# A block-sparse attention and MLP kernel: a new order of operations, the row table built first, and other bytes for outputs that nobody reads

## The chip, the cores and the metric

The kernel runs on one core of one Trainium2 chip. The time is the device time of one execution in microseconds (us). The five engines of the core run their own instruction streams and wait for each other by semaphores: TensorE (PE, whose weight loads are listed apart as PEld), VectorE (DVE), ScalarE (ACT), GpSimd (POOL) and SyncE (SP), which here only issues transfers.

## The reference

Four batches of eight heads, 768 positions of 64 columns. Blocks of 32 positions attend to their neighbours, to the first and last block, and to three blocks drawn at random for each row of blocks; the first and last block attend to everything. The result, 3072 rows of 512 columns, goes through a two-layer network with a leaky activation whose slope is given for each of the 2048 inner columns.

```python
mask = np.abs(blk_i - blk_j) <= window
mask = mask | (blk_i == 0) | (blk_j == 0) | (blk_i == n_blocks - 1) | (blk_j == n_blocks - 1)
for qb in range(n_blocks):
    for kb in sampled_blocks[qb]:
        mask[qb * block:(qb + 1) * block, kb * block:(kb + 1) * block] = True
scores = np.where(mask, scale * np.matmul(q, k.transpose(0, 1, 3, 2)), -1000000000.0)
attn = softmax(scores); x = rows of np.matmul(attn, v)
h = x @ w_in
out = (np.maximum(h, 0.0) + alpha * np.minimum(h, 0.0)) @ w_out
```

## The kernel before

All matmuls take float16 operands; a float32 number is carried as a high and a low half (names ending in hi and lo, or gh and gl), so that a product takes three matmuls. Scales that keep the halves in range come from norms of the inputs, worked out on the chip.

**Units.** The attention is cut into 48 units U0 to U47: for each batch b and each of six query tiles t, two halves c of four heads. Five tiles are sparse; the sixth (t = 5; U10, U11, U22, U23, U34, U35, U46, U47) holds the rows that attend to everything and is called dense. A unit is a chain: scores on PE (L741) into one of three banks; `emit_bias` on DVE (L823: mask, scale and row minimum nm); the exponential on ACT (L830); high half of the probabilities p_hi (L451 on ACT, L453 on DVE, L455 on POOL); low half p_lo (L459 on DVE, L461 and L462 on POOL); a transposing DMA `pt<-ph` issued by SP (L875 sparse, L879 dense); and the product with the values on PE (L741, `a<-v,pt` and the like). Then `evict`: the row scale, x_mul (L883), its halves, and the transposing DMA `x<-xn` (L900).

**Keys and values.** For each batch they are normed, split into halves and transposed (`keys<-ph`, L594); the blocks drawn at random come by POOL's copies (L736) and by an indirect DMA on POOL (L697, `vr<-scr,vidx`). The indices vidx come from a table of five columns called vrow (row number and comparisons, L411 to L420) and vpick. Queries: `qf` is loaded, squared and summed on ACT (`emit_q_sq`, L447), scaled on DVE (L440, L443: uq, sq), split (qn), transposed (`qt<-qn`, L525), and a second copy with halves swapped is made by a DMA `qs<-qt`; dense scores need both.

**The network.** Twelve chunks M0 to M11 of 256 rows follow the units: for each of eight steps j, up (L1352; M0 in float32, L1340), the activation on DVE (L1362, L1366), its high half on ACT (L1375) and low half on POOL (L1381), and down (L1402) into an output bank; then out (L1412) and a store. Up and down write two and two banks. The norm of w_in and w_out is worked out with chains of small matmuls and of `diag` (L548, DVE), which ends in `otot` (L1202), `mm` (L1209) and s_wo (L443).

**What sets the order.** Every step is an operation of a `Plan`, numbered as the program text comes to it, 2492 in all. `Plan.run` goes through a table `ORDER` (L70 to L164), whose words name an engine and a number (D for DVE, A for ACT, G for POOL, S for SP, P for PE); it hands out buffers in that order, and each engine issues in that order without going around a waiting instruction. Only the code ahead of the plan (L287 to L375) and the constants are placed by the text.

**Outputs that nobody reads.** ACT's squares (L447) and DVE's `diag` are wanted for their sums alone. ACT writes the squares into the first bytes of a tile called rawp (under the name spare), or for the first query tile into phs[0], a buffer for probabilities; `diag` writes the first 128 columns of rawp, the same bytes as spare.

## Time and profile before

| | |
|---|---|
| Median of three runs | 773.38 us (767.51 to 775.49) |
| The profiled execution | 775.92 us, of which the span of instructions is 773.7 us |
| Mean granted clock of PE | 0.976 |
| PE busy | 697.6 us (90%), 9978 instructions |
| DVE busy | 533.7 us (69%), 1377 |
| ACT busy | 371.3 us (48%), 838 |
| POOL busy | 475.6 us (61%), 848 |
| Chain that ended last | PE 68%, DVE 11%, DMA 10%, issue 5%, others below 3% each |

The page has the span in 40 slices; PE is busy 3, 4, 5, 7, 7, 7 tenths in the first ones and nine tenths from the tenth on with two slices at eight. DVE stands at eight and nine tenths in the first twelve slices, and lower after that. An execution is 2.2 us longer than its span of instructions. Matmuls are pipelined, so that the durations of neighbours overlap; sums of PE's time are taken from the stretches that a view gives as one piece. An idle time in square brackets is that of the engine just before the row's instruction, with what ended it.

### The profile page before, as it was taken

Reading aid. Unit: us, or ns where it says so; the run is one execution under the profiler, and the core shown is the slowest. Engines: PE = TensorE matmul, PEld = TensorE weight load, DVE = VectorE, ACT = ScalarE, POOL = GpSimd, SP = SyncE. Lnnn points to the kernel's source line nnn. Section 1 sums busy time; section 2 is a strip of 40 time slices with the busy share of each in tenths; the row PEclk is TensorE's granted clock in tenths of the full one; section 3 lists DMA queues with packets and bytes.
Section 4 is the critical chain, followed back from the end, with each engine's and each line's share of the span. In section 5 each row is a group of like instructions: output and inputs, shape, how many; then the busy total and the mean of one; then the engine's idle time right before and its main releaser. Section 6 shows DMA issues by size and latency. Waiting matters only on the chain.

```text
span 773.7 us, 25323 instructions
## 1 busy us (share of the span) xinstructions
PE 697.6 (90%) x9978; PEld 490.8 (63%) x9978; DVE 533.7 (69%) x1377; ACT 371.3 (48%) x838; POOL 475.6 (61%) x848
## 2 busy tenths in 40 slices
PE   3457799899989999999999989999998999999997
PEld 2345588456657757668667566577674677676673
DVE  3888899889887654878776757589754547586130
ACT  3546668773744433466434455366531533343211
POOL 5359545564677787758768767475785677345121
PEclk9976899999999999999999999999998999999999
DMA  8987769777897999999997999998984878756200
GB/s 235 297 252 219 222 152 233 171 179 151 167 190 217 188 205 179 202 222 191 170 210 191 178 202 210 188 195 166 184 226 129 154 161 149 165 98 113 65 1 28
DMA packets 284710, 136.48 MB, mean 176 GB/s; under 512 B 216992, under 2 KB 272432, under 8 KB 284592
## 3 DMA queue, kind: packets, MB, share of 16 engines
q1 hardware_dynamic: 256064, 98.74, 64.2%
q0 software_dynamic: 5792, 18.36, 8.8%
q10 hardware_dynamic: 22736, 17.77, 8.3%
q8 instruction: 78, 1.28, 0.7%
q14 instruction: 40, 0.33, 0.1%
HBM read 70.86 MB, written 12.58 MB: 108 GB/s over the span
## 4 chain that ended last, share of the span: by engine, by line
PE 68%; DVE 11%; DMA 10%; issue 5%; POOL 2%; ACT 2%; SPq 1%; another core or an unknown queue 0%; POOLq 0%; ACTq 0%; DVEq 0%
PE o L1402 25%; PE h L1352 24%; PE s L741 6%; PE a L741 5%; PE h L1340 4%; DMA pt<-ph 3%; DVE ph L459 2%; DMA vf<-in_k_dram 2%; DMA qs<-qt 1%; DVE e L823 1%; DMA qf<-in_q_dram 1%; DVE wi L1166 1%; DMA vn<-scr 1%; POOL gl L1381 1%; DMA keys<-ph 1%
## 5 line engine op out<-in xcount | busy, mean ns | idle before, releaser
L1352 PE MATMUL h<-x,wi 128*128 128x256 f16 x2112 | 242.9, 274 | 2.1 <-DMA x<-xn 1.2
L1352 PEld LDWEIGHTS <-wi 128*128 128x128 f16 x2112 | 205.8, 98 | 34.5 <-issue 3.0
L1402 PE MATMUL o<-wo,gh 128*128 128x512 f16 x728 | 216.7, 379 | 1.2 <-ACT g L1412 1.2
L1381 POOL TENSOR_TENSOR gl<-g,gh 128x512 f16<-128x512 f32 x91 | 109.1, 1205 | 101.4 <-ACT gh L1375 92.7
L736 POOL COPY keys<-keys 128x128 f16 x480 | 130.2, 320 | 23.7 <-ACT keys L605 15.2
L1402 PE MATMUL o<-wo,gl 128*128 128x512 f16 x364 | 138.0, 379 | 0.0
L830 ACT ACTIVATE e<-e,nm 128x256 f32<-128x256 f32 x160 | 79.9, 500 | 104.5 <-DVE nm L823 97.5
L1362 DVE SCALAR_TENSOR_TENSOR g<-h,am 128x512 f32<-128x512 f32 x96 | 65.8, 686 | 86.3 <-PE h L1352 66.1
L1402 PEld LDWEIGHTS <-gh 128*128 128x128 f16 x728 | 68.7, 98 | 76.5 <-issue 3.0
L1375 ACT CAST gh<-g 128x512 f16<-128x512 f32 x91 | 55.4, 611 | 116.1 <-DVE g L1366 66.9
L823 DVE CUSTOM_DVE_ANT_0 e<-s,bias,cs 128x256 f32<-128x256 f32 x160 | 73.3, 477 | 33.5 <-POOL ph L462 15.9
L697 POOL DMA_INDIRECT vr<-scr,vidx x80 | 79.5, 994 | 24.5 <-issue 19.0
L741 PEld LDWEIGHTS <-pt 128*32 128x32 f16 (+1 forms) x4416 | 58.7, 96 | 31.3 <-issue 21.5
L1366 DVE SCALAR_TENSOR_TENSOR g<-h,gsc,g 128x512 f32<-128x512 f32 x96 | 72.1, 751 | 3.4
L741 PE MATMUL s<-keys,qt 128*32 128x192 f16 (+2 forms) x864 | 69.2, 254 | 4.5 <-DVE nm L823 2.9
L741 PE MATMUL s<-keys,qs 128*32 128x192 f16 (+2 forms) x864 | 69.9, 253 | 1.9 <-DMA qs<-qt 1.9
L1402 PEld LDWEIGHTS <-gl 128*128 128x128 f16 x364 | 35.6, 98 | 43.4 <-POOL gl L1381 0.5
L461 POOL TENSOR_SCALAR e<-e 128x512 f32<-128x512 f32 (+1 forms) x38 | 27.7, 729 | 57.0 <-ACT ph L451 30.3
L459 DVE SCALAR_TENSOR_TENSOR ph<-e,ph 128x512 f16<-128x512 f32 (+1 forms) x62 | 59.6, 967 | 2.0 <-ACT ph L451 1.6
L462 POOL TENSOR_TENSOR ph<-e,ph 128x512 f16<-128x512 f32 (+1 forms) x38 | 50.6, 1332 | 3.2
L451 ACT ACTIVATE ph<-e 128x512 f16<-128x512 f32 (+1 forms) x69 | 47.7, 693 | 4.6 <-DMA pt<-ph 2.1
L741 PE MATMUL a<-vr,pt 128*32 128x64 f16 x1920 | 39.4, 199 | 6.4 <-issue 6.3
(216 smaller groups left out, 963.1 us busy)
## 6 DMA issues: line engine op xcount, KB each, us to landing
vn<-scr SPq DMA_DIRECT2D x60, 192.0 KB
wo<-in_moe_w_in_dram SPq DMA_DIRECT2D x15, 512.0 KB
qs<-qt SPq DMA_DIRECT2D x40, 128.0 KB
vf<-in_k_dram SPq DMA_DIRECT2D x18, 256.0 KB
vf<-in_v_dram SPq DMA_DIRECT2D x16, 256.0 KB
scr<-v SPq DMA_DIRECT2D x16, 256.0 KB
vn<-scr ACTq DMA_DIRECT2D x20, 192.0 KB
qf<-in_q_dram SPq DMA_DIRECT2D x14, 256.0 KB
```

The source lines that it names most:

```text
L459: nc.vector.scalar_tensor_tensor(dst, src, scale, hi, ALU.mult, ALU.subtract)
L697: nc.gpsimd.indirect_dma_start(dst[:n], None, T["scr", b].rearrange("s h a -> s (h a)"), bass.IndirectOffsetOnAxis(ap=vidx[:n, i : i + 1], ...
L736: nc.gpsimd.tensor_copy(kr[:, :, g, r], kt[:, :, bass.ds(i * HB2, HB2)])
L741: nc.tensor.matmul(dst, lhs, rhs, start=start, stop=False, skip_group_check=True)
L823: nc.vector.tensor_tensor_reduce(e_view(u, h // 2)[:, h % 2, :], T["sp", u, h], bias[:, t], scale=T["cs", b, t][:, c : c + 1], scalar=3.0e ...
L830: nc.scalar.activation(e, e, AF.Exp, bias=T["nm", u, h], scale=-1.0, accum_out=su_of(u, h))
L1352: nc.tensor.matmul(ph[:, i, :], win(k, f, ct), x[:, l, ct, cols], start=(m == 0), stop=(m == len(terms) - 1))
L1362: nc.vector.scalar_tensor_tensor(g, ph, 0.0, a2, ALU.min, ALU.mult)
L1366: nc.vector.scalar_tensor_tensor(g[:, i : i + 2], ph[:, i : i + 2], sc, g[:, i : i + 2], ALU.mult, ALU.add)
L1375: nc.scalar.copy(T["gh", c, j, half], g)
L1381: nc.gpsimd.tensor_tensor(T["gl", c, j, half], g, T["gh", c, j, half], ALU.subtract)
L1402: nc.tensor.matmul(T["o", c, t], g[:, i, a : a + P], wout(w, f), start=(f == 0 and m == 0), stop=(f == NF - 1 and m == 2),)
```

## The change

Three things are changed; what is computed, and with which instructions, stays the same.

- **The table.** All 2492 words of `ORDER` are given anew. Some operations go to another engine: 47 from ACT to DVE and 45 back, 37 from POOL to DVE and 35 back, 35 loads from ACT to SP and 26 back, 14 from ACT to POOL and 8 back.
- **The row table.** The two POOL and nine DVE instructions that build vrow leave the planned operation `o_vidx` for the code ahead of the plan, and the five DVE instructions that are left in it form the operation.
- **Bytes that are thrown away.** The first query's squares go into the tile qn that is allocated there, not into phs[0]; `diag` writes bf16 into columns of rawp behind those that ACT's squares fill.

```diff
--- before.py
+++ after.py
@@ -68,99 +68,99 @@
 ORDER = """
-S289 S274 S26 A307 S272 S273 A308 D309 A312 D313 P12 D13 S290 G0 D1 D4 A8 S359 D27 A28 G2 S14 P275 D276 D277 P278 D279 S291 P314 P316 D29 A42 D317 S74
...
+A307 S273 S274 A272 S26 P275 A308 D309 D312 D313 G0 D1 S291 D27 A28 D29 S234 S289 D276 D277 P278 A290 D3 S359 S14 S232 S74 D279 D286 A283 G287 S42
...
 """
@@ -297,6 +297,18 @@
     rawp = cpool.tile([P, 3 * W2 // 4], I32, name="rawp")
     nc.scalar.dma_start(rawp[:, : NBLK * NR * 2], smp.partition_broadcast(P))
     sraw = rawp[:, : NBLK * NR * 2].rearrange("p (a r w) -> p a r w", r=NR, w=2)
+    vrow = cpool.tile([P, 5], F32, name="vrow")
+    row, below, m1, m2, tmp = (vrow[:, i : i + 1] for i in range(5))
+    nc.gpsimd.iota(row[:KR], pattern=[[0, 1]], base=0, channel_multiplier=1, allow_small_or_imprecise_dtypes=True)
+    nc.gpsimd.iota(row[KR:], pattern=[[0, 1]], base=0, channel_multiplier=1, allow_small_or_imprecise_dtypes=True)
+    for r, n in ((slice(0, KR), KR // 2), (slice(KR, P), HB2)):
+        nc.vector.tensor_scalar(below[r], row[r], n - 0.5, None, ALU.is_ge)
+        nc.vector.scalar_tensor_tensor(row[r], below[r], -float(n), row[r], ALU.mult, ALU.add)
+    nc.vector.tensor_scalar(m1, row, HB2 - 0.5, None, ALU.is_ge)
+    nc.vector.tensor_scalar(m2, row, 2 * HB2 - 0.5, None, ALU.is_ge)
+    nc.vector.scalar_tensor_tensor(row, below, float(SP2), row, ALU.mult, ALU.add)
+    nc.vector.tensor_tensor(tmp, m1, m2, ALU.add)
+    nc.vector.scalar_tensor_tensor(row, tmp, -float(HB2), row, ALU.mult, ALU.add)
     ident16 = cpool.tile([P, P], F16, name="ident16")
     nc.gpsimd.tensor_copy(ident16, ident)
 
@@ -321,7 +333,6 @@
     sidx = wi[:1, 0, 3 * P : 3 * P + NBLK * NR].bitcast(I32).rearrange("p (a r) -> p a r", r=NR)
     vidx = cpool.tile([P, TS * NG4], I32, name="vidx")
     vpick = cpool.tile([P, TS * NG4, NR], F32, name="vpick")
-    vrow = cpool.tile([P, 5], F32, name="vrow")
     spack = cpool.tile([1, TS * NG4 * NR // 2], I32, name="spack")
     bias = cpool.tile([P, TS, CS], BF16, name="bias")
     dbias = cpool.tile([P, S], BF16, name="dbias")
@@ -407,17 +418,6 @@
     o_regs = plan.op(-11, {"POOL": 3.5}, lambda: emit_regs(nc.gpsimd, "g"), [o_pack])
 
     def emit_vidx():
-        row, a, m1, m2, tmp = (vrow[:, i : i + 1] for i in range(5))
-        nc.gpsimd.iota(row[:KR], pattern=[[0, 1]], base=0, channel_multiplier=1, allow_small_or_imprecise_dtypes=True)
-        nc.gpsimd.iota(row[KR:], pattern=[[0, 1]], base=0, channel_multiplier=1, allow_small_or_imprecise_dtypes=True)
-        for r, n in ((slice(0, KR), KR // 2), (slice(KR, P), HB2)):
-            nc.vector.tensor_scalar(a[r], row[r], n - 0.5, None, ALU.is_ge)
-            nc.vector.scalar_tensor_tensor(row[r], a[r], -float(n), row[r], ALU.mult, ALU.add)
-        nc.vector.tensor_scalar(m1, row, HB2 - 0.5, None, ALU.is_ge)
-        nc.vector.tensor_scalar(m2, row, 2 * HB2 - 0.5, None, ALU.is_ge)
-        nc.vector.scalar_tensor_tensor(row, a, float(SP2), row, ALU.mult, ALU.add)
-        nc.vector.tensor_tensor(tmp, m1, m2, ALU.add)
-        nc.vector.scalar_tensor_tensor(row, tmp, -float(HB2), row, ALU.mult, ALU.add)
         v = [vpick[:, :, x] for x in range(NR)]
         nc.vector.tensor_tensor(v[2], v[2], v[1], ALU.subtract)
         nc.vector.tensor_tensor(v[1], v[1], v[0], ALU.subtract)
@@ -425,7 +425,7 @@
         nc.vector.scalar_tensor_tensor(v[0], v[2], m2, v[0], ALU.mult, ALU.add)
         nc.vector.tensor_scalar(vidx, v[0], float(HB2), row, ALU.mult, ALU.add)
 
-    o_vidx = plan.op(P_REG, {"POOL": 3.0}, emit_vidx, [o])
+    o_vidx = plan.op(P_REG, {"DVE": 1.1}, emit_vidx, [o])
     o_r = plan.op(-9, {"DVE": 2.0}, mask_random, [o])
     o_d = plan.op(0, {"DVE": 0.75}, mask_dense, [o])
     o_bias = [plan.op(-8 + 5 * t, {"ACT": 0.5, "POOL": 0.6}, lambda e, t=t: spread_picked(e, t), [o_r]) for t in range(TS)]
@@ -497,7 +497,10 @@
 
     def emit_q_sq(b, t):
         T["ssq", b, t] = new_small("ssq", n=4)
-        early = phs[0].rearrange("p a b c -> p (a b c)").bitcast(U8) if (b, t) == (0, 0) else None
+        early = None
+        if (b, t) == (0, 0):
+            T["qn", b, t] = wt("qn", [P, H, 2, D], F16)
+            early = T["qn", b, t].rearrange("p h a d -> p (h a d)").bitcast(U8)
         squares(T["qf", b, t].rearrange("p h d -> p (h d)"), T["ssq", b, t], early)
 
     def emit_q_scale(b, t):
@@ -511,7 +514,8 @@
         nc.vector.tensor_scalar(cs, T["rk", b][:, a:z], T["uq", b, t], -(2.0**-100), ALU.mult, ALU.min)
 
     def emit_q_hi(e, b, t):
-        T["qn", b, t] = wt("qn", [P, H, 2, D], F16)
+        if ("qn", b, t) not in T:
+            T["qn", b, t] = wt("qn", [P, H, 2, D], F16)
         times(e, T["qn", b, t][:, :, 0, :], T["qf", b, t], T["sq", b, t])
 
     def emit_q_lo(b, t):
@@ -546,7 +550,7 @@
 
     def diag(src, acc):
         nc.vector.tensor_tensor_reduce(
-            rawp[:, :P].bitcast(F32), src, ident, scale=1.0, scalar=0.0, op0=ALU.mult, op1=ALU.add, accum_out=acc,
+            rawp[:, P:].bitcast(BF16), src, ident, scale=1.0, scalar=0.0, op0=ALU.mult, op1=ALU.add, accum_out=acc,
         )
 
     def emit_sq_diag(key, b, c):
@@ -976,11 +980,11 @@
         plan.tag = f"Q{b}{t}"
         fb, nb = plan.buf("qf"), plan.buf("qn")
         o = plan.op(pl, LQ, lambda e: emit_load_q(e, b, t), gate, [fb], dma=1.6, n=1 + (t == TS))
-        o = plan.op(prio, {"ACT": 0.8}, lambda: emit_q_sq(b, t), [o], [], [fb])
+        o = plan.op(prio, {"ACT": 0.8}, lambda: emit_q_sq(b, t), [o], [nb] if (b, t) == (0, 0) else [], [fb])
         o = plan.op(prio, {"DVE": 0.27}, lambda: emit_q_scale(b, t), [o])
         for c in range(NQ):
             o_cs[b, t, c] = plan.op(prio, {"DVE": 0.08}, lambda c=c: emit_cs(b, t, c, c + 1), [o, o_rk[b, c]])
-        o = plan.op(prio, {"POOL": 0.7, "ACT": 0.63, "DVE": (0.36, 0)}, lambda e: emit_q_hi(e, b, t), [o], [nb], [fb])
+        o = plan.op(prio, {"POOL": 0.7, "ACT": 0.63, "DVE": (0.36, 0)}, lambda e: emit_q_hi(e, b, t), [o], [] if (b, t) == (0, 0) else [nb], [fb] + ([nb] if (b, t) == (0, 0) else []))
         o = plan.op(prio, {"DVE": (0.79, 0)}, lambda: emit_q_lo(b, t), [o], [], [nb, fb])
         qtbuf[b, t], qsbuf[b, t] = plan.buf("qt"), plan.buf("qs")
         if (b, t) < (0, Q_PE):
```

In the changed kernel L426 to L497 keep their numbers, and later lines stand three or four further down: L525 is L529 there, L548 is L552, L741 is L745, L823 is L827, L875 is L879, L900 is L904, L1202 is L1206.

VectorE at the program's start, and where the row table stood before. Before, behind the weights' arithmetic (wi, wo) of the first 50 us:

```order
L1161 SCALAR_TENSOR_TENSOR wi<-wo,wi 128x512
L511 TENSOR_SCALAR cs<-rk,uq 128x1
L414 TENSOR_SCALAR vrow<-vrow 96x1
L415 SCALAR_TENSOR_TENSOR vrow<-vrow 96x1
L414 TENSOR_SCALAR vrow<-vrow 32x1
L415 SCALAR_TENSOR_TENSOR vrow<-vrow 32x1
L416 TENSOR_SCALAR vrow<-vrow 128x1
L417 TENSOR_SCALAR vrow<-vrow 128x1
L418 SCALAR_TENSOR_TENSOR vrow<-vrow 128x1
L419 TENSOR_TENSOR vrow<-vrow 128x1
L420 SCALAR_TENSOR_TENSOR vrow<-vrow 128x1
L422 TENSOR_TENSOR vpick<-vpick 128x20
```

In the changed kernel, from VectorE's first memset on:

```order
L287 MEMSET ones 128x128
L305 TENSOR_SCALAR vrow<-vrow 96x1
L306 SCALAR_TENSOR_TENSOR vrow<-vrow 96x1
L305 TENSOR_SCALAR vrow<-vrow 32x1
L306 SCALAR_TENSOR_TENSOR vrow<-vrow 32x1
L307 TENSOR_SCALAR vrow<-vrow 128x1
L308 TENSOR_SCALAR vrow<-vrow 128x1
L309 SCALAR_TENSOR_TENSOR vrow<-vrow 128x1
L310 TENSOR_TENSOR vrow<-vrow 128x1
L311 SCALAR_TENSOR_TENSOR vrow<-vrow 128x1
L440 TENSOR_SCALAR uq<-ssq 128x1
```

All nine vrow instructions moved from behind the weights to ahead of the first query.

VectorE at the end of the norm of w_out, with the numbers of the buffers. Before:

```order
L548 ISA rawp_131,osum_190<-o0_120,ident_122 128x128
L548 ISA osum_190 128x1
L440 TENSOR_SCALAR uq_2391<-ssq_2356 128x1
L443 TENSOR_SCALAR sq_2392<-uq_2391 128x1
L1202 TENSOR_REDUCE otot_2396<-osum_190 128x1
L1209 TENSOR_REDUCE mm_2402<-o1_121 128x1
L440 TENSOR_SCALAR mu_2403<-mm_2402 128x1
L443 TENSOR_SCALAR s_wo_192<-mu_2403 128x1
L453 TENSOR_SCALAR wo_136<-wo_136,s_wo_192 128x512
```

In the changed kernel:

```order
L552 ISA rawp_131,osum_201<-o0_120,ident_122 128x128
L552 ISA osum_201 128x1
L1206 TENSOR_REDUCE otot_2380<-osum_201 128x1
L1213 TENSOR_REDUCE mm_2383<-o1_121 128x1
L440 TENSOR_SCALAR mu_2384<-mm_2383 128x1
L443 TENSOR_SCALAR s_wo_203<-mu_2384 128x1
L827 ISA e1_81,nm_2392<-s1_115,bias_163,cs_1807 128x256
```

A query's two scale steps (uq, sq) no longer stand between the last `diag` and otot, and the first split of w_out (L453) is no longer VectorE's; it stands on POOL.

SyncE's queue at the query of the dense unit U34 (qt_77 and qs_79). Before:

```order
L875 DMA_TRANSPOSE pt_86<-ph_138 128x8x128
L875 DMA_TRANSPOSE pt_84<-ph_141 128x8x128
L525 DMA_TRANSPOSE qt_77<-qn_75 128x8x128
L594 DMA_TRANSPOSE keys<-ph_140 128x8x128
L900 DMA_TRANSPOSE x_89<-xn_88 128x8x128
L479 DMA qs_79<-qt_77 64x1024 x2
L875 DMA_TRANSPOSE pt_83<-ph_138 128x8x128
```

In the changed kernel:

```order
L529 DMA_TRANSPOSE qt_77<-qn_75 128x8x128
L479 DMA qf_74<-in_q_dram 128x8x64
L479 DMA vn_104<-scr_7079 48x4x512 x2
L879 DMA_TRANSPOSE pt_84<-ph_151 128x8x128
L479 DMA qs_79<-qt_77 64x1024 x2
L904 DMA_TRANSPOSE x_89<-xn_88 128x8x128
L479 DMA vn_103<-scr_7079 48x4x512 x2
L598 DMA_TRANSPOSE keys<-ph_152 128x8x128
```

The swap `qs<-qt` now stands ahead of the transposes of x and of the keys, and behind the loads of a query and of values.

## Rows read from the trace of the kernel before

**Rows 1.** Three windows: length, busy PE, PEld, DVE, ACT, POOL (count), PEclk, DMA, GB/s.

```profile
9.20:101.70 92.50, 55.13 (x1006) 45.02 (x1006) 78.43 (x250) 52.06 (x96) 50.34 (x128) 0.85 0.80 241
101.70:773.70 672.00, 642.35 (x8974) 445.66 (x8973) 455.07 (x1127) 317.02 (x739) 418.79 (x685) 0.99 0.83 167
586.10:592.90 6.80, 5.80 (x60) 4.03 (x61) 0.00 (x0) 0.00 (x0) 5.20 (x15) 0.50 0.48 142
```

**Rows 2.** Waits until 102 us, VectorE and TensorE: us in total, times, longest.

```profile
DVE uq L440 <- ACT ph L447: 8.2, 1, 8.2
...
PE h L1176 <- DVE iu L440: 3.8, 1, 3.8
```

**Rows 3.** Timeline of VectorE at 50 us: start, us, engine, line, operation.

```profile
49.75 0.14 DVE L414 TENSOR_SCALAR vrow<-vrow 96x1 f32<-96x1 f32 x1
...
51.08 0.18 DVE L422 TENSOR_TENSOR vpick<-vpick 128x20 f32<-128x20 f32 x1
```

**Rows 4.** TensorE's waits from 102 us to the end.

```profile
PE a L741 <- issue: 6.0, 13, 0.5
PE a L741 <- DMA pt<-ph: 5.0, 5, 2.1
...
PE s L741 <- DMA qs<-qt: 1.9, 1, 1.9
...
PE s L741 <- DVE nm L823: 1.2, 2, 0.6
...
PE o L1239 <- DVE wo L453: 0.5, 1, 0.5
```

**Rows 5.** Timeline at the end of w_out's norm, VectorE.

```profile
138.77 0.15 DVE L440 TENSOR_SCALAR uq<-ssq 128x1 int32<-128x1 int32 x1
...
139.02 0.15 DVE L1202 TENSOR_REDUCE otot<-osum 128x1 f32<-128x8 f32 x1
...
140.46 1.99 DVE L453 TENSOR_SCALAR wo<-wo,s_wo 128x512 f16<-128x512 f32 x1
```

**Rows 6.** Timeline of SyncE's queue ahead of U34.

```profile
483.36 3.03 SPq L900 DMA_TRANSPOSE x<-xn  x1
486.48 1.18 SPq L479 DMA_DIRECT2D qs<-qt  x2
```

**Rows 7.** TensorE's timeline: first product with values of U27 and of U47.

```profile
448.09 0.27 PE L741 MATMUL a<-vn,pt 128*32 128x64 f16 x12 [2.05 <-DMA pt<-ph]
...
709.66 0.41 PE L741 MATMUL a<-v,pt 128*128 128x64 f16 x8 [0.66 <-DMA pt<-ph]
```

**Rows 8.** U27's low half: VectorE's timeline, POOL's, and the line's durations (ns).

```profile
438.40 3.70 DVE L459 SCALAR_TENSOR_TENSOR ph<-e,ph 128x512 f16<-128x512 f32 x1
...
438.69 2.28 POOL L1381 TENSOR_TENSOR gl<-g,gh 128x512 f16<-128x512 f32 x2
...
L459 DVE SCALAR_TENSOR_TENSOR ph<-e,ph x62: 676/732/3700, 113.2 to 704.4; 128x512 f16<-128x512 f32 x41, 128x768 f16<-128x768 f32 x21
```

**Rows 9.** Timeline of VectorE and TensorE at M5's fourth step.

```profile
410.76 0.75 DVE L1366 SCALAR_TENSOR_TENSOR g<-h,gsc,g 128x512 f32<-128x512 f32 x1
...
410.78 0.61 PE L1402 MATMUL o<-wo,gh 128*128 128x512 f16 x2
```

**Rows 10.** Chain that ended last, 535 to 600 us: start, length, what.

```profile
546.12 2.62 PE h L1352 x24
548.74 0.53 PE a L741 x18
549.27 2.59 PE o L1402 x12
...
552.68 1.01 PE s L741 x40
...
582.69 0.49 issue
```

**Rows 11.** U47's first head: timeline of TensorE's last scores, of SyncE's transposes.

```profile
687.95 0.33 PE L741 MATMUL s<-keys,qs 128*128 128x384 f16 x1
...
703.81 2.55 SPq L879 DMA_TRANSPOSE pt<-ph  x2
```

More of the change, by code (lines that the diff above doesn't have):

```diff
@@ new lines @@
+G2 D45 P250 A251 P255 P366 P22 D298 G318 D256 D257 P258 D259 A288 D23 S285 S54 D311 D262 S78 D55 D41 D79 D264 D265 A260 D261 S98 A367 A56 S62 D57 G8
+D99 P321 D322 A80 D362 A100 P266 A267 P58 D263 P46 D59 P60 S305 D101 D63 A299 D77 P270 S66 D61 D67 D68 S86 D81 S411 P268 A269 D87 D47 A102 A271 G337
+S302 D69 S282 D88 P368 P82 D83 S90 A412 A64 D329 A330 A369 D331 D306 D413 S320 D416 D417 A332 A323 D324 A325 D103 D91 D65 A104 P339 D340 A341 D342
+D414 P34 D35 P333 A334 D335 G319 P70 D71 P36 A92 D105 A7 P24 S115 D25 D347 A343 D363 S125 P326 A348 D327 D349 G370 G389 P373 D328 P12 D374 P344 A350
@@ new lines @@
+D13 D345 D346 A375 D376 S121 D381 A382 P72 G422 D93 D73 S111 S131 D126 A127 A377 P351 D352 D353 P391 D399 P84 D383 S338 A400 D85 G441 P418 D419 P336
+P420 D401 A384 P385 D122 D123 P106 D107 P108 D112 A402 D392 A421 P378 A386 S464 A9 G371 A393 D109 D394 P425 D128 D132 D89 D415 P94 D426 A395 D124 D379
+A113 D114 D380 D133 A465 A427 D428 P354 S390 P396 A372 A397 D355 D116 S141 P443 A117 D466 D398 D387 S155 P403 A404 G469 D470 D118 D405 D95 S594 D356
+D407 P473 A474 D444 D134 S171 A445 G423 P129 D130 D37 P357 A358 D446 P48 A429 D433 A434 P388 D435 A447 P430 A431 D432 S145 S135 P406 D408 S151 A436
@@ new lines @@
+P771 D768 D889 D922 G928 P930 A914 D915 A1003 S720 A893 D894 S867 A916 P772 A896 S644 D897 D938 S958 A917 G918 A939 A864 P732 S919 A769 D1004 P733
+D735 A923 A868 D869 A736 D940 S959 D737 P870 A924 A890 D871 A872 D773 G960 G1007 A774 D1008 G770 S738 D891 A878 P776 P777 D925 G775 P963 P783 S898
+G979 G1011 P787 A941 D875 A892 D873 D879 D876 A880 D971 A972 S895 S874 S877 G910 S1053 D784 A785 P791 S926 G786 P778 D899 D931 A932 D1005 D788 A789
+A942 D943 D933 D973 P981 D982 A983 P796 S1009 G790 D792 A793 G794 A934 S911 A779 S780 P801 S929 D1006 D984 S944 S1010 A935 G936 D797 P806 A1054 G1030
@@ new lines @@
+P927 D1055 A781 A985 D1056 S937 D964 A965 D966 A967 D946 A1058 D1059 D802 P795 A974 A975 D976 D968 A798 G961 D969 P800 P1014 S970 S1149 A986 P805 D989
+A990 D987 P945 G799 P810 P811 D991 A992 D997 D993 G994 D807 S962 G1062 P816 A803 G804 D1015 A1016 D1017 P1032 A1150 D1022 A1023 S1060 D1151 A808 G809
+S977 D947 A948 D1057 G1154 S995 D1024 G949 G1012 D1033 D812 S988 S980 S950 D817 A1018 A818 D1019 P815 P820 G819 A813 P978 P996 D998 A999 D1000 G814
+G1020 S1061 A1034 D1035 A1036 A1025 P821 P1065 S1013 S782 S1001 D1040 D1155 S1156 A1041 D1026 G1027 D1042 A1043 D1048 S1382 A1044 G1045 S1386 G1063
@@ new lines @@
+P822 A825 D1037 D1073 P1105 D1106 A1107 G1108 P1109 P1113 D1038 D1110 P1118 G1081 A1074 D1075 P1083 D1104 A1111 D1114 P1123 S1200 A1201 G1158 D1066
+A1067 D1068 A1076 S826 S1039 S1021 D1084 D1202 A1069 S1028 D1077 P1029 G1205 S1157 A1115 S1046 D1206 A823 P1117 G1112 P1122 D1078 D1091 A1383 A824
+D1124 A1085 A1384 A1070 D1086 A1092 D1093 D1204 S1031 S1207 P1161 D1119 D1071 A1387 A1125 A1120 S1420 A1087 D1153 D1088 G1177 S1079 A1385 P1047 D1049
+D1388 D1089 A1094 G1116 P1127 G1126 P1389 D1390 G1121 G1159 S1064 D1394 A1421 D1099 D1095 G1096 A1050 G1051 S1072 S1455 P1128 P1133 P1132 D1152 D1162
@@ L164 @@
+A2450 G2451 D2462 P2466 P2460 A2458 A2454 G2455 P2465 D2467 P2471 P2476 A2463 G2464 D2472 P2481 A2473 G2459 D2482 G2474 P2470 A2468 G2469 P2475 A2483
+G2484 P2480 P2485 D2477 A2478 G2479 P2486 P2487 A2488 S2489 A2490 S2491
 """
```

162 lines of the change are left out of this document (70 added, 92 removed).

## The prediction

> **What bounds the kernel now.** I read the windows first, cut at 9.2 us (where VectorE leaves its first wait) and at 101.7 us (where M0's first up begins) [rows 1]. The reader is to see two regimes. From 101.7 on TensorE is busy 642.35 of 672.0 us at a clock of 0.99: there only what TensorE waits for counts, 29.6 us in all, and VectorE (455) and POOL (419) have room. Before that TensorE is busy 55.13 of 92.5 us, and VectorE 78.43: it works off a list, and has 14.1 us of gaps. So I next read the waits: VectorE's and TensorE's up to 102 us [rows 2], TensorE's from there on [rows 4]. Then I went to the place of each wait in the timeline and in the changed order. As both orders hold the same operations, and TensorE's list is nearly full, the time can fall by the waits that go, by a shorter list of VectorE in the head, and rise by waits that the new order makes. That is what the sum counts.
>
> **The row table.** Nine VectorE instructions ran from 49.75 to 51.08, 1.33 us [rows 3], in the stretch that VectorE bounds, and shortly ahead of the step L440 for which TensorE waited 3.8 us [rows 2]. In the change they stand right behind the first memset, where VectorE sat idle 8.2 us for ACT's squares L447 [rows 2]; the work hides there whole. If the cover were gone it would cost the 1.3 us again. Bounds: 0, if another wait in the head ends last, and -1.3. I take **-1.3**, since the other work that stands in front of TensorE's first up on VectorE is the same within 1 us, counted from both orders.
>
> **The thrown-away bytes.** `diag` and ACT's squares no longer share bytes. Where `diag` waited for them at the end of w_out's norm, the one behind it waited for TensorE anyway; alone it is worth 0. Bound above: the 0.7 below.
>
> **The end of w_out's norm.** In the order, uq and sq leave the place between the last `diag` and otot: 139.02 - 138.77 = 0.25 us on TensorE's path [rows 5]. The first split L453 of w_out, 1.99 us on VectorE [rows 5], goes to POOL; TensorE waited 0.5 us for it [rows 4]. The sum is **-0.7**. It could be 0 if POOL is later with that split than VectorE was.
>
> **The swap at U34.** TensorE waited 1.9 us for `qs<-qt`, once [rows 4]. SP issued it at 486.48, behind the transpose of x that held it 3.03 us, from 483.36 [rows 6]. In the changed order it stands ahead of that transpose and of a keys transpose, so it can go some 3 us earlier, more than the wait: **-1.9**. New ahead of it are a query load and a load of values; they are issues on the same queue. If one waits for its buffer by as much as x's transpose took, the term is 0.
>
> **Waits for transposed probabilities.** TensorE waited five times, 5.0 us [rows 4]. The longest, 2.05 at U27 [rows 7], goes back to VectorE's p_lo at 438.40, which took 3.70 us where the median is 0.732 [rows 8]: 2.97 us too long. POOL ran two low halves gl of the network from 438.69 on, 2.28 us [rows 8]. In the new order U27's first mask steps and p_lo stand further ahead, before the activation of two of M's steps, so that p_lo should not meet those gl: **-2.0**. Bound: 0. Of the others, 5.0 - 2.05 - 0.66 = 2.3 us lie at U23, U29 and U35, where TensorE's work between scores and product grows by 2.6 us or more (counted from the order, each piece with the length it has in the trace): **-2.3**, the lower bound being 0. The 0.66 at U47 [rows 7] stays in the term on late heads. The two waits of dense scores for nm, 1.2 us [rows 4], are at U10; the work ahead of the first grows by 3 us, of the second it doesn't: **-0.6**, of 0 to -1.2.
>
> A rule speaks against this term. The Trainium skill ("SBUF — State Buffer", Who interferes with whom) says that a VectorE instruction with two inputs from SBUF and a GpSimd instruction that reads SBUF lock each other out for the whole of one instruction. The trace agrees as far as the pair of 3.70 and 2.28 us goes [rows 8]. By the rule the 2.0 us come back wherever the new order lets such a pair meet ahead of a short lead, and the sum would be 2.0 higher; by the row it happened at one place, which the order parts.
>
> **A new wait at M5.** Before, TensorE did one set of sparse scores (1.01 us) and then a down (2.59) between two ups whose second needs a bank that the activation frees [rows 10]. In the new order the scores alone stand between them. The activation L1366 started at 410.76 and takes 0.75, so ends at 411.51; TensorE was through with the scores at 410.78 [rows 9]. It would wait 411.51 - 410.78 = **+0.7**.
>
> **The late dense heads.** The last dense heads lose cover. For U47's first head TensorE's scores ended at 687.95 + 0.33 = 688.28, its two transposes were issued at 703.81 [rows 11], and the product began at 709.66 after a wait of 0.66 [rows 7]: 21.4 us. In the new order there lie three downs, one up, four dense products and six dense scores between: 3 x 2.59 + 2.62 + 4 x 0.53 [rows 10] + 6 x 0.33 [rows 11] = 14.5 us. If the chain of that head takes as long as before, TensorE waits 21.4 - 14.5 = 6.9 us; if the chain is only as long as its instructions, 0, as 15.5 of the 21.4 us passed before the transposes were issued, most of it in queues. I take about a third, **+2.5**, because VectorE is busy only 455 of 672 us there [rows 1] and its order was laid anew too.
>
> **What stays.** TensorE's waits for instructions, 13 before products, 6.0 us [rows 4]; the work of all engines that changed hands (some 120 operations each way, which cancel in number).
>
> **The sum.** -1.3 - 0.7 - 1.9 - 2.0 - 2.3 - 0.6 + 0.7 + 2.5 = -5.6. From the profiled execution, whose span of 773.7 and 2.2 us around it make 775.9, that gives 770.3. That execution stands 2.5 above the median of 773.4, so on the scale of the median it is 767.8; I say **768.0 us**.
>
> **Rivals.**
>
> The gains only move (24%). TensorE's list is the same; a wait removed at one place comes back at the next, for example a p_lo that meets POOL's gl elsewhere, or U47's head at its 6.9. For it: VectorE and POOL keep their load, and the leads at the late heads fall. Against it: most of the waits stand alone, with several us of free work behind them. The sum is then -5.6 + 2.0 + (6.9 - 2.5) = +0.8, or **774 us**; with only one of the two it is 770 to 772.
>
> A stall of instructions goes (20%). At 582.69 begins a series of waits of TensorE for its own instructions, 0.49 us each [rows 10], seven until 588.2, 3.4 us together, the larger part of the 6.0 [rows 4]. Right behind it, from 586.1 to 592.9, the granted clock is 0.50, which is 1.2 GHz [rows 1]: 6.8 us of work that at 2.4 GHz is half, 3.4 us more. If the new order puts another mix of products at that place, and the stall does not form, 6.8 us go beyond the sum: **761 us**. For it: no such series stands at another unit, so it hangs on the place. Against it: nothing in the order says that the stream's supply is any different, and the same products still follow each other; a second one could form.
>
> The head is late (14%), the other side. The first loads come in another order: in SP's queue a key tile comes ahead of the last value tiles, and two value tiles go to ACT's queue. VectorE's gaps are 92.5 - 78.43 = 14.1 us [rows 1], and the transfers move 241 GB/s there, against 167 later. If the first pieces arrive so that VectorE waits as long again, all of it delays the first up, since nothing in the head hides it: 767.8 + 14.1 = **782 us**. It decides from about 13 us on. For it: the clock stands at 0.85 in the head, so TensorE has no reserve either. Against it: TensorE's and VectorE's work ahead of the first up is the same in sum, and the weights' arithmetic can be done whenever its tile is there.
>
> **How the numbers follow.** The forecast has 42%; it is the likeliest, and with each term at its bounds it runs from 764 to 773. The rivals hold 24, 20 and 14%. The range of **757 to 780** takes in the two rivals that gain or give back, with 4 us more below for leads that are longer at other units, and stops short of the late head. A measurement of this kernel can tell about 1% from no change, 7.7 us. Faster by over 1% (below 765.6): the stall's 20% and about a third of the forecast's 42%, **0.34**. Slower by over 1% (above 781.1): most of the late head, **0.12**. Within 1%: **0.54**.
>
> **What would show it.** In the changed profile: VectorE's vrow rows before 2 us, and the first up at about 100 us instead of 101.6; no wait for `qs<-qt` at U34; waits for `pt<-ph` below 3 us without the late heads, and a p_lo near 0.73 us at U27; a wait of 0.5 to 1 us at M5's fourth step; a wait for `pt<-ph` at U47's first head, of 0 to 7 us. A low clock or a series of instruction waits at another place, and a first up at 105 us or later, would make the forecast wrong.

## The result

The changed kernel runs in 761.49 us (median of 13 runs, 755.98 to 766.82), the kernel before in 770.54 (13 runs, 766.25 to 775.49). The ratio is 0.988, with an interval of 0.9849 to 0.9912: 9 us less, 7 to 12 by the interval. The forecast was 768.0 in a range of 757 to 780. The time lies in the range and on the forecast's side; the size was underestimated, and the class that it falls in, faster by over 1%, had been given 0.34, less than the 0.54 of "within 1%". The profiled execution of the changed kernel took 759.19 us with a span of 757.4. Medians are of all executions, ratios and intervals (95%) only of those within 1.5% of the fastest one of their kernel in the same rounds, so that a ratio can differ from that of two medians.

The three runs shown before the change had a median of 773.38; ten more put it at 770.54. The execution that was profiled then (775.92) is 5.4 us above that. Part of what its trace shows is therefore not the kernel's usual course, and the experiments tell which part. Of the experiments' profiled executions one, e4's, stands 10.3 us above its kernel's median; it is left out where traces are compared, unless it is named.

The page of the changed kernel, for [rows 1]: busy time, and TensorE and its granted clock in 40 slices.

```profile
PE 691.7 (91%) x9978; PEld 491.3 (65%) x9978; DVE 530.4 (70%) x1380; ACT 364.7 (48%) x829; POOL 486.2 (64%) x855
...
PE   2467599799999999899989989999999999999997
...
PEclk9997989999999999999999999999999999999999
```

From the page of the kernel before, TensorE and VectorE in the same slices:

```profile
PE   3457799899989999999999989999998999999997
DVE  3888899889887654878776757589754547586130
```

TensorE is at seven tenths in the fourth and fifth slice and at eight or nine from the sixth on, but for the last. VectorE is at eight or nine from the second to the twelfth, which ends at 232 us, and mostly lower behind it.

The same work is done. TensorE is busy 691.7 us where it was 697.6, which is the clock, and VectorE has 3 us less, GpSimd 11 us more.

Windows of the changed kernel: length, then busy PE, PEld, DVE, ACT, POOL (with counts), granted clock, DMA share, GB/s. The cuts are the first up of M0 (99.4), that of M2 (229.7) and the last down of M11 (749.7). TensorE has done the same work at each of these points in both orders.

```profile
99.40:229.70 130.30, 123.72 (x1582) 86.67 (x1579) 117.31 (x281) 88.76 (x186) 84.88 (x123) 0.99 0.83 172
229.70:749.70 520.00, 509.25 (x7388) 356.89 (x7385) 335.59 (x845) 221.62 (x542) 347.31 (x574) 1.00 0.86 169
```

The same two stretches of the kernel before, which the window from 101.7 to 773.7 us of [rows 1] had taken as one:

```profile
101.60:235.40 133.80, 125.26 (x1583) 86.97 (x1579) 120.56 (x292) 90.68 (x188) 76.93 (x114) 0.99 0.85 185
235.40:766.40 531.00, 514.43 (x7385) 357.67 (x7384) 334.61 (x836) 225.12 (x550) 341.86 (x571) 0.99 0.83 164
```

This is the reading that the prediction lacked. From 101.6 to 235.4 us VectorE is busy 120.56 of 133.8 us, 90%, nearly as much of its time as TensorE; behind it 334.61 of 531, 63%. The changed kernel has 11 instructions and 3.25 us less for VectorE in that stretch and 8 us more for GpSimd, and the stretch is 3.5 us shorter.

TensorE's waits of the changed kernel from 99 us on, for [rows 4]: us in total, times, longest.

```profile
PE a L745 <- DMA pt<-ph: 3.5, 5, 1.4
PE a L745 <- issue: 2.2, 2, 2.0
PE s L745 <- DVE nm L827: 1.6, 1, 1.6
PE o L654 <- DVE otot L1206: 1.3, 1, 1.3
PE h L1356 <- DVE g L1370: 1.3, 2, 0.6
PE o L1242 <- ACT sid L451: 1.2, 1, 1.2
PE o L1243 <- DVE wo L453: 1.0, 1, 1.0
...
PE s L745 <- POOL keys L740: 0.9, 2, 0.7
PE h L654 <- DVE vtot L662: 0.8, 1, 0.8
...
PE s L745 <- DMA qs<-qt: 0.3, 1, 0.3
```

`qs<-qt` has gone from 1.9 us to 0.3, at another unit, and vtot from 2.4 to 0.8; the wait for the activation's bank (L1370) is not there in the kernel before; otot has not moved (1.2 to 1.3).

### The profile page after: what moved, and what is told of

Read it like the earlier page. It is cut to its first block, busy times and chain, and to the rows that moved or that the text cites. A ratio compares the mean times of both kernels' runs of the same rounds, so it can differ in the third digit from the quotient of the medians.

```text
span 757.4 us, 25365 instructions
## 1 busy us (share of the span) xinstructions
PE 691.7 (91%) x9978; PEld 491.3 (65%) x9978; DVE 530.4 (70%) x1380; ACT 364.7 (48%) x829; POOL 486.2 (64%) x855
## 4 chain that ended last, share of the span: by engine, by line
PE 68%; DVE 11%; issue 6%; DMA 4%; POOL 3%; SPq 2%; ACT 2%; POOLq 1%; DVEq 0%; ACTq 0%
PE o L1406 28%; PE h L1356 27%; PE s L745 6%; PE a L745 5%; DMA pt<-ph 2%; POOL keys L740 1%; DVE wo L1170 1%; DVE e L827 1%; SPq L883 1%; PE h L1344 1%; DVE ph L459 1%; DVE g L1366 1%; DVE wi L459 1%; DVE g L1370 1%; DVE wo L1158 1%
## 5 line engine op out<-in xcount | busy, mean ns | idle before, releaser
L701 POOL DMA_INDIRECT vr<-scr,vidx x80 | 81.6, 1020 | 21.7 <-issue 18.3
L827 DVE CUSTOM_DVE_ANT_0 e<-s,bias,cs 128x256 f32<-128x256 f32 x160 | 73.0, 477 | 29.9 <-PE s L745 28.4
L745 PE MATMUL s<-keys,qt 128*32 128x192 f16 (+2 forms) x864 | 70.2, 251 | 9.1 <-POOL keys L740 4.8
L1370 DVE SCALAR_TENSOR_TENSOR g<-h,gsc,g 128x512 f32<-128x512 f32 x96 | 72.1, 751 | 3.4
L745 PEld LDWEIGHTS <-pt 128*32 128x32 f16 (+1 forms) x4416 | 58.2, 96 | 24.5 <-issue 15.6
L745 PE MATMUL s<-keys,qs 128*32 128x192 f16 (+2 forms) x864 | 69.2, 250 | 0.3 <-DMA qs<-qt 0.3
L459 DVE SCALAR_TENSOR_TENSOR ph<-e,ph 128x512 f16<-128x512 f32 (+1 forms) x62 | 53.5, 867 | 10.5 <-ACT ph L451 9.9
L841 DVE CUSTOM_DVE_ANT_0 e<-s,dbias,cs 128x384 f32<-128x384 f32 x64 | 38.0, 612 | 18.6 <-PE s L745 16.6
L745 PEld LDWEIGHTS <-qs 128*32 128x32 f16 (+1 forms) x864 | 36.6, 100 | 15.4 <-issue 8.5
L745 PEld LDWEIGHTS <-qt 128*32 128x32 f16 (+1 forms) x864 | 38.6, 100 | 11.5 <-issue 3.4
```

What stands on the lines that cost most here:

```text
L459: nc.vector.scalar_tensor_tensor(dst, src, scale, hi, ALU.mult, ALU.subtract)
L701: nc.gpsimd.indirect_dma_start(dst[:n], None, T["scr", b].rearrange("s h a -> s (h a)"), bass.IndirectOffsetOnAxis(ap=vidx[:n, i : i + 1], ...
L745: nc.tensor.matmul(dst, lhs, rhs, start=start, stop=False, skip_group_check=True)
L827: nc.vector.tensor_tensor_reduce(e_view(u, h // 2)[:, h % 2, :], T["sp", u, h], bias[:, t], scale=T["cs", b, t][:, c : c + 1], scalar=3.0e ...
L1370: nc.vector.scalar_tensor_tensor(g[:, i : i + 2], ph[:, i : i + 2], sc, g[:, i : i + 2], ALU.mult, ALU.add)
```

## The experiments

All but the last are timed over five rounds against the kernel before on the same chip. Most of them put the two tables together: up to some word of TensorE the one order, behind it the operations that are left in the other's order. The words are the same 2492 in each, so nothing is done twice or left out.

### The small edits alone, and the table alone

```diff
 e1: the code of the changed kernel
-(the new table)
+(the old table)   ... D3 ...
 e2: the code of the kernel before
-(the old table)
+(the new table)   ... G3 ...
```

> The old table of orders; only the row table goes first and the unread outputs get bytes of their own. If the nine row-table instructions were on the path of the head, 1.3 us less than before, so a ratio of 0.998. Rival: another wait in the head ends last, ratio 1.000. The trace tells of both: the first up of M0 at 100.3 us or at 101.6 us. TensorE's order is that of before, so if the series of instruction waits at U36 hangs on the place in the program it stands there again, 3.4 us of waits and a granted clock near 0.5 right behind it; if it belonged to that one execution it is gone or shorter.

> The new table with the row table and the shared bytes as before. If the table brings all but 1.3 us of the 9 us (1.2%) that the change is worth, the ratio to before is 0.990. Rival: the new table was laid out for the row table standing first, so that its nine instructions in the middle of the head delay a load or a gather, and the ratio is 0.995 or more.

The small edits gave 767.91 us, ratio 1.0006 (0.997 to 1.0043); the table alone 760.54, ratio 0.9884 (0.9836 to 0.9933). So the gain is the table's. The 1.3 us of the row table, 0.2%, lie inside either interval, and are neither shown nor excluded. In the traces the first up of M0 began at 98.2 us with the old table and the row table early, where it was 101.6; but with the same old head and the row table early it lay between 98.2 and 101.9 in six executions, so that the place of nine instructions can't be read out of one. (The two kernels with the row table late have 101.6 and 101.3, the twelve with it early 99.6 on the mean; this points the forecast's way, and two are too few.)

The stall of the prediction's second rival is settled by the first of these kernels. TensorE's order is that of before. Window of e1 over U36 and what follows, where the kernel before had a series of instruction waits and a clock of 0.50 [rows 1, 10]:

```profile
578.00:592.00 14.00, 14.00 (x308) 9.79 (x307) 9.84 (x32) 6.38 (x18) 11.67 (x22) 1.00 0.88 193
```

TensorE is busy all the 14 us at the full clock. Seven executions with the old order at U36 were profiled, and the one shown before the change is the only one with the stall. It belonged to that execution, as its 5.4 us above the median already suggested. Of the 13 instruction waits of 6.0 us in [rows 4], none comes back in another execution of the old order.

### Front and tail

```diff
 e3: the new table to M7's last down, then the old
-... P1888 A1895 A2044 D2074 A2075 ...
+... P1888 S2119 A2044 A2045 D2046 ...
 e4: the old table to M7's last down, then the new
-... P1888 G1896 A1899 A2052 G2053 ...
+... P1888 D2115 A1899 G1896 G1900 ...
```

> The new order up to the last down of M7 (563 us), the old order of what is left from there on, with both small edits. The traces put 7.5 us of the gain ahead of that point. If the waits that went are the gain, about 763 on the scale of before at 770.5, a ratio of 0.990. If the stall at U36 was there in every execution and is the larger part of what executions gain, the old rest brings it back and the ratio is 0.997 or more.

> The old order up to the last down of M7 (570 us), the new order from there on, with both small edits. In the two profiles that stretch gained 9.2 us, of which 6.8 us are the stall at U36 and the low clock behind it. If the stall stands in every execution of the old order, the ratio is 0.988; if it was a thing of the one execution that was profiled, only the 2 us of waits go, and the 1.3 us of the row table, ratio 0.996.

The new front gave 761.62 us, ratio 0.9891 (0.9843 to 0.9938); the new tail 769.56, ratio 1.0002 (0.9962 to 1.0041). All that can be measured lies ahead of M7's last down; e4 expected 0.988 or 0.996, and neither came. From there to M11's last down the traces take 187.0 to 187.4 us in the old order (the one with the stall aside: 196.0) and 186.8 to 187.9 in the new one. The late heads, for which the prediction put 2.5 us, cost nothing in the traces (a timing can't tell 0.3%).

### Head, the stretch from 100 to 235 us, and the rest

```diff
 e5: the new table to M0's fifth up, then the old
-... D138 A173 D174 G559 P139 A489 ...
+... D138 A173 D174 A442 D597 P440 ...
 e6: old to M0's first up, new to M2's first up, then old
-... P518 A442 D158 D144 P522 ...
+... P518 S171 S135 D468 D450 ...
...
-... P783 S898 G979 G1011 P787 ...
+... P783 D1005 D1006 S1009 A898 ...
 e7: old to M2's first up, then new
-... P783 G875 D876 A874 S895 ...
+... P783 D954 A774 D925 G775 ...
 e8: new to M3's last down, old to M5's last down, then new
-... P1144 A1213 A1214 A1145 S1146 ...
+... P1144 P1227 A1213 A1405 A1506 ...
...
-... P1377 P1638 S1601 A1589 D1590 ...
+... P1377 D1659 A1589 S1601 A1624 ...
 e11: old to M0's first up, then new
-... P518 A442 D158 D144 P522 ...
+... P518 S171 S135 D468 D450 ...
```

> The new order up to M0's fifth up (about 110 us), the old order of all that is left, with both small edits. In the three profiles of the old front the first up began at 101.6, 98.2 and 100.1 us, in the three of the new front at 101.3, 99.8 and 99.4: no difference, so a ratio of 1.000. The rival, that the head is where the change pays (the two profiles shown first differ by 2.2 us there, and all that VectorE does is counted), gives 0.995 or less.

> The old order up to M0's first up, the new order from there to M2's first up (TensorE has done the same work at both points in both orders), the old order behind. The stretch took 133.8, 135.1 and 140.0 us in the old front's profiles and 129.1, 130.6 and 130.3 in the new one's, 6.3 us less on the mean, of which 4 are waits of TensorE (for the value norm of batch 1, for row minima of U10, for copied keys) and 2 its clock. If that stretch is the gain, the ratio is 0.992. If the leads gained there have to be carried on by the new order behind, or began in the head, the ratio is 0.997 or more.

> The old order up to M2's first up, the new one behind it: the swap at U34, U27's low half, the waits at U22, U23 and U35 and all the late heads, and nothing of the stretch 100 to 235 us. By the waits of my prediction (swap 1.9, U27 2.0, others) a ratio of 0.993 would follow. By the stretches of the six profiles, where old and new are level from M2's first up to M5's last down and 1 us apart up to M7's, it is 0.998 to 1.000.

> The new order, but the old one between M3's last down (334 us) and M5's last down (446 us), where the new order waits at U22, U23 and for M4's and M5's activations, 1.5 us more than the old one on the mean of three profiles each. If the stretches can be put together freely the ratio is 0.986, a little below the new order's 0.988; if the old order needs leads there that the new one has not laid, 0.990 or more.

> The old order up to M0's first up, the new one for all that follows, with both small edits. The profiles put no part of the gain in the head, so a ratio of 0.988, as with the whole table. If the new order of the head lays leads for the stretch behind it, 0.993 or more.

| | median us | ratio to before (interval) |
|---|---|---|
| e5, new head | 769.37 | 1.0043 (1.0003 to 1.0084) |
| e6, new from 100 to 235 us | 765.14 | 0.9941 (0.9891 to 0.9991) |
| e7, new behind 235 us | 770.89 | 1.0028 (0.9977 to 1.008) |
| e8, new with the old middle | 763.14 | 0.9952 (0.992 to 0.9985) |
| e11, old head, new behind | 765.07 | 0.9947 (0.9913 to 0.9982) |

Only the stretch from 100 to 235 us gains by itself, 0.6% of the 1.2; the interval of e6 holds both numbers that were expected. The waits that the prediction counted behind it, 3.0 us in sum with its two losses, bring nothing that can be measured (e7). My expectation of e8, better than the whole new table, was not met: the old middle costs 0.7% by the ratios and 0.2% by the medians, which is no more than 1.7 us and not clear of noise. And e11 gains less than the whole table, as its second branch had it, though the head alone gains nothing (e5).

Medians of all executions, sorted by which order holds in the head (to M0's first up) and in the stretch to M2's first up, whatever stands behind:

| | old stretch | new stretch |
|---|---|---|
| old head | 769.6 (124; before, e1, e4, e7) | 765.1 (24; e6, e11) |
| new head | 769.4 (12; e5) | 761.6 (37; changed, e2, e3, e8) |

The kernel before had medians from 768.7 to 770.5 in the four groups of rounds, so that differences below 2 us say nothing here. The new stretch is worth 4.5 us beside the old head and nearly 8 beside the new one; the new head is worth nothing beside the old stretch and 3.5 us beside the new one (2.8 by the means, with an interval of 1.0 to 4.5). So about half of the gain hangs on head and stretch being laid together; that it hangs on both is at the edge of what these numbers can tell, and no trace shows where those 3 us are.

The lengths of the stretches in the profiles, each by the order that held in it (without e4, and in the last row without the execution that had the stall):

| stretch | old order | new order |
|---|---|---|
| start to M0's first up | 98.2 to 101.9, mean 99.8 (7) | 98.6 to 101.3, mean 99.9 (6) |
| to M2's first up | 133.7 to 139.3, mean 136.7 (5) | 128.6 to 130.6, mean 129.7 (6) |
| to M5's last down | 213.2 to 220.0, mean 215.4 (6) | 215.6 to 221.3, mean 217.8 (6) |
| to M7's last down | 114.7 to 119.2, mean 117.3 (6) | 115.5 to 120.4, mean 118.5 (7) |
| to M11's last down | 187.0 to 187.4, mean 187.2 (6) | 186.8 to 187.9, mean 187.3 (6) |

One stretch parts the two orders without overlap, by 7 us. (The runs e9 and e10, below, mix order and engines in that stretch and are not counted in its row; e5, whose new head ends 10 us into it, is counted as old.) The means sum to 3 us less, not 9: executions of one kernel differ by 10 us and more, and those that were profiled lay up to 7.5 us below their kernel's median and up to 6 above.

What TensorE waits for in that stretch, in the old order; e7's execution:

```profile
PE s L752 <- POOL keys L747: 4.2, 4, 2.3
PE h L661 <- DVE vtot L669: 2.2, 1, 2.2
```

The scores of U12 wait for keys that GpSimd copies: 0.9 to 4.2 us in the five old executions, 0.5 to 0.9 in the six new ones. V10's norm waits 2.0 to 2.7 us there, 0.85 each time in the new order. U10's two waits for row minima (0.5 to 0.9 each) are gone, but for 0.3 us in e2, and so is the one at U14 (0.4 to 1.7, in four of the five). What ended each of them is an instruction of VectorE or GpSimd. Over these executions, means of the old order and of the new: TensorE stands 10.7 and 6.0 us, and is busy 126.0 and 123.7, at a granted clock of 0.96 to 0.99 and of 0.97 to 1.00. So of the 7 us nearly 5 are waits and 2 are the clock. VectorE is busy 121.1 and 118.5 us and idle 15.6 and 11.2.

### Order or engines

```diff
 e9: the old order, the new table's engines from M0's first to M2's first up (42 words)
-... A599 ... D484 ... D560 ... G563 ...
+... D599 ... G484 ... A560 ... D563 ...
 e10: the new order, the old engines there (42 words)
-... D599 ... A560 ... A501 ...
+... A599 ... D560 ... D501 ...
```

> The old order everywhere, with both small edits; only between M0's first up and M2's first up the 40 or so operations that the new table gives to another of VectorE, ScalarE and GpSimd go there (18 leave VectorE, 14 come to it). VectorE is busy there 120 to 122 us of 134 to 140 in four profiles of the old order and 117 to 119 of 129 to 131 in five of the new one, GpSimd 77 and 84. If the shorter list of VectorE is what shortens the stretch, it takes about 132 us and the ratio is 0.996. If the gain is in the order of its operations, the stretch stays at 135 to 140 us and the ratio is 1.000 or more, since the old order is not laid for these engines.

> The new order everywhere, but in the stretch between M0's first up and M2's first up the engines of the old table, for the same operations as in the run before this one, the other way round. If the engines are the gain, the stretch takes 133 us or more and the ratio is 0.992 or above; if the order is, it stays at about 130 and the ratio is 0.988.

778.81 us, ratio 1.0107 (1.0045 to 1.0168), and 784.51, ratio 1.018 (1.0126 to 1.0234). Read singly, e9 would put the gain in the order and e10 in the engines; both stretches are longer than in either original. So neither engines nor order bring the gain by themselves, each without the other makes the stretch longer than it was. Windows of e9, then of e10:

```profile
98.60:242.70 144.10, 130.18 (x1581) 88.72 (x1578) 123.07 (x287) 88.20 (x184) 83.76 (x121) 0.95 0.82 172
```

```profile
98.60:250.80 152.20, 131.13 (x1580) 89.63 (x1579) 122.88 (x287) 91.48 (x189) 80.99 (x117) 0.93 0.68 148
```

VectorE does the same 123 us in both and has the rest idle, 21 and 29 us, against 13 in the two windows shown first, and 10 to 19 in all executions of the two orders. In e9 it was to have the shorter list, 117 to 119 us, and has 123, more than in the old order (120 to 122). So what a shorter list is worth by itself was not tested. In e10 it stands behind halves that another engine now makes late; VectorE's waits in that window:

```profile
DVE ph L466 <- ACT ph L458: 9.3, 4, 7.6
DVE e L848 <- POOL ph L469: 2.7, 1, 2.7
DVE ksum L576 <- ACT rawp L454: 2.5, 1, 2.5
```

One high half on ScalarE alone kept it for 7.6 us. TensorE, which then waits, also loses clock: 0.95 and 0.93 against 0.99. So in this stretch an operation that changes its engine has to change its place with it.

### One word: the swap at U34

```diff
-... G1714 S1762 G1681 A1675 ...
+... G1714 S1762 S1763 G1681 A1675 ...
```

> The old order with both small edits, and one word moved: the swap of U34's query goes right behind its transpose in SyncE's queue, ahead of the transposes of keys and of x. TensorE waited there for it in each of four profiles of the old order, 1.1 to 3.4 us. If those transposes were what held it, the wait is gone or below 0.3 us; if the query's own transpose is what comes late, it stays above 1 us. Its worth in time is below what a timing tells; it is read from the trace.

One execution, 764.97 us. SyncE's queue in e12, for [rows 6]:

```profile
479.52 1.71 SPq L536 DMA_TRANSPOSE qt<-qn  x1
484.93 1.13 SPq L486 DMA_DIRECT2D qs<-qt  x2
486.15 1.33 SPq L605 DMA_TRANSPOSE keys<-ph  x1
487.58 2.52 SPq L911 DMA_TRANSPOSE x<-xn  x1
```

TensorE's waits in e12 from 400 to 570 us, all that there are:

```profile
PE a L752 <- DMA pt<-ph: 3.7, 4, 2.1
PE o L1413 <- POOL gl L1392: 0.6, 1, 0.6
```

The wait for `qs<-qt` is gone, as expected. It is a weak proof, from one execution: with the old order at U34 it was 1.9, 1.2 and 1.1 us in before, e1 and e5, and 3.4 in e4, but 0 in e6 and 0.2 in e9. How long the transpose of x held the queue does not part these: 3.0 us in before, but 1.4 in e1 as in e6 and e9. In those with a wait it ended 8.7 to 12.1 us behind the swap's issue; in e12 the swap had landed 5.1 us behind it, and its issue stood at most 2 us further ahead of the scores. So in e12 the transfer itself was the quicker one, and why is not shown. The swap now waits itself for the query's transpose, until 484.93, with both other transposes queued behind it, and still TensorE waits for neither.

## Why the prediction was right and wrong

**What bounds the kernel.** Failed in one step. "From 101.7 on TensorE is busy ... VectorE (455) and POOL (419) have room" took an average over two stages with different limits. Cut at M2's first up, VectorE is busy 90% in the first part and 63% in the second. The first part is where the only piece that gains by itself lies, and the prediction had two small terms there, -0.7 and -0.6; V10's norm, U12's keys and U14's scores it put at nothing without naming them, nearly 4 us of waits by the means of the experiments.

**The row table, -1.3.** The cover was there: in the changed kernel VectorE does the nine instructions while it waits for the first query, as its timeline shows.

```profile
1.43 0.15 DVE L305 TENSOR_SCALAR vrow<-vrow 96x1 f32<-96x1 f32 x1 [0.45 <-POOL vrow L302]
...
2.69 0.16 DVE L311 SCALAR_TENSOR_TENSOR vrow<-vrow 128x1 f32<-128x1 f32 x1
9.38 0.15 DVE L440 TENSOR_SCALAR uq<-ssq 128x1 int32<-128x1 int32 x1 [6.53 <-ACT qn L447]
```

The wait behind them is 6.5 us where it was 8.2 [rows 2]. Whether 1.3 us came of it in time was not shown.

**The thrown-away bytes, 0.** Near: the wait for otot is 1.2 us in before and 0.9 in each execution of the old order with the bytes moved; in the new order it is 1.3 with them (changed kernel) and without (e2).

**The end of w_out's norm, -0.7.** Wrong, by its size. The 0.25 us of uq and sq are gone, and the split that TensorE waited for is GpSimd's; but otot is waited for 1.3 us in the new order, and the next split on VectorE costs 1.0 in the changed kernel. In sum the three waits (otot, sid, wo) are 2.5 to 3.5 us in the new order, 2.1 to 2.9 in the old. The term is 0 at best.

**The swap, -1.9.** Right by place, and the cause fits: no wait at U34 in any of the seven executions of the new order there, and none with one word moved. By size it is 0 to 1.9 (3.4 in e4), since the old order doesn't pay in every execution. In the changed kernel the swap stands at 475.28, ahead of both transposes:

```profile
475.28 1.32 SPq L479 DMA_DIRECT2D qs<-qt  x2
476.69 1.32 SPq L904 DMA_TRANSPOSE x<-xn  x1
...
483.58 1.25 SPq L598 DMA_TRANSPOSE keys<-ph  x1
```

**U27's low half, -2.0.** Right by cause. In all eight profiled executions where the old order stood there, p_lo took 3.70 to 3.72 us, and TensorE waited 2.1 to 3.2 us (e4 and e8 are among them). In the changed kernel the pair is apart; VectorE's timeline, GpSimd's, and the line's durations:

```profile
431.10 0.69 DVE L459 SCALAR_TENSOR_TENSOR ph<-e,ph 128x512 f16<-128x512 f32 x1
```

```profile
427.27 2.28 POOL L1385 TENSOR_TENSOR gl<-g,gh 128x512 f16<-128x512 f32 x2
```

```profile
L459 DVE SCALAR_TENSOR_TENSOR ph<-e,ph x62: 674/693/1909, 117.8 to 694.3; 128x512 f16<-128x512 f32 x38, 128x768 f16<-128x768 f32 x24
```

The longest low half is 1.9 us instead of 3.7. But 1.3 to 2.3 us came back just there, as instruction waits at U28 or late transposes at U26, in each of six executions of the new order, where the old has 0.4 at the most. So about half of the term is left, as the rival "the gains only move" had it; that the one wait makes the other is not shown.

**U23, U29 and U35, -2.3.** Wrong: nothing went. TensorE's waits for transposes at U22, U23, U29 and U35 are 1.9 to 3.7 us in the old order (six executions, mean 2.4) and 2.5 to 3.9 in the new one (six, mean 3.1). What failed is the measure: I counted TensorE's work between scores and product, and not how much later the transposes themselves are issued in the new order. At U23's third head they go out 10.6 and 11.9 us behind the scores in the kernel before, 18.7 and 20.0 in the changed one.

**U10, -0.6.** Better than forecast: both waits are gone in the changed kernel, 1.2 us.

**M5, +0.7.** Right to the tenth: 0.63 us in each execution of the new order. Waits of the same kind that I did not see are U20's scores (1.6 to 2.7 us for a row minimum, in every one) and M4's fourth up (up to 0.6, in four).

**The late heads, +2.5.** Wrong; the lower end, 0, held. In the changed kernel U47's first head is done with its scores at 678.45, has its transposes issued 8.7 us later, where it was 15.5, and its product does not wait: it begins 14.5 us behind the scores, the lead that I had counted. TensorE's timeline, then SyncE's, for [rows 11]:

```profile
678.12 0.33 PE L745 MATMUL s<-keys,qs 128*128 128x384 f16 x1
```

```profile
687.16 2.54 SPq L883 DMA_TRANSPOSE pt<-ph  x2
```

So the chain fits into 14.5 us, and what was longer before was queues, as the prediction itself gave for its lower bound. The third of 6.9 us that I took as a wait was not there.

**The rivals.** "A stall of instructions goes" named 761 us, next to what was measured, and for a cause that the runs exclude: the stall was not part of the usual time, so nothing could be gained by its going. Its "no such series stands at another unit, so it hangs on the place" took one execution for the kernel. "The head is late" is excluded: the head is level. The forecast's 5.6 us against 9 came out near by luck: terms that failed on both sides (-2.3, -0.7 and +2.5) made up for each other, and the main gain, 7 us by the profiles and 0.7 to 8.4 by the timing of e6, was in none of them but for U10's 0.6. The bounds of the forecast, 764 to 773, also don't follow from its terms: with each at its upper end the sum is 0.7 + 6.9, which is 781.

**What stays open.** Which moves between 100 and 235 us make the gain: engines and order each fail without the other, and finer pieces were not tried. Whether the waits that are shorter there come of VectorE's shorter list or of its order. And why the whole is worth 1.2% where the only piece that gains alone is worth 0.6%: that the new head lays leads for the stretch fits e5, e6 and e11, and is argued and not shown.

## What to carry to other kernels

Cut the profile where the load of the second-busiest engine changes before saying who bounds what: an engine at 69% over the whole was at 90% for 134 us, and most of what TensorE waited for there was its work or GpSimd's. Take a wait as the kernel's own only when it comes back in another execution, above all when the profiled one is some us above the median. Change the engine of an operation only together with its place: here the new engines in the old order cost 1.1%, the old engines in the new order 1.8%.
